# Sketch attention feeding a SiLU MLP on one core: another order of loads and of work, one sixteen-tile pass for the query sketches, and token-major last chunks

## The chip, the cores and the metric

The kernel runs on one core of one Trainium2 chip. The metric is the device time of the whole kernel in microseconds. For the kernel before, 13 runs are shown: median 99.57 us, lowest 98.78 us, highest 100.95 us. In the program's names, PE is TensorE (PEld its weight loads), DVE is VectorE, ACT is ScalarE, POOL is GpSimd, and SP is SyncE, which here only issues DMAs.

## The reference, cut to what matters

```python
def phi(x):                                   # x: 4 x 4 x 1088 x 32, r = 8
    a = np.einsum('rd,bhsd->bhsr', S1, x)
    b = np.einsum('rd,bhsd->bhsr', S2, x)
    return np.einsum('bhsi,bhsj->bhsij', a, b).reshape(*x.shape[:-1], r * r)
q_p, k_p = phi(q), phi(k)
kv  = np.einsum('bhsf,bhsd->bhfd', k_p, v)
z   = np.sum(k_p, axis=2)
num = np.einsum('bhsf,bhfd->bhsd', q_p, kv)
den = np.einsum('bhsf,bhf->bhs', q_p, z)[..., None] + 1e-06
x   = (num / den).transpose(0, 2, 1, 3).reshape(4 * 1088, 128)
h   = x @ w_in                                # w_in 128 x 2048
out = (h * sigmoid(h)) @ w_out                # w_out 2048 x 128, all float32
```

The attention has no softmax: keys and queries are turned into 64 products of two 8-long sketches, and the rest is sums and matrix products. Four batches of 1088 tokens give 4352 rows for the MLP.

## The kernel before, in words

**Two kinds of work share the engines.** The MLP part (`moe_tasks`) takes chunks of 512 or 256 tokens. For each 1024 columns of hidden values PE multiplies x by w_in into one of two double PSUM banks H (line 718), ACT applies SiLU from H to one of eight SBUF tiles G (line 722, 68 times in all), and PE multiplies G by w_out into one of four single PSUM banks B, summing over the hidden dimension (line 729). With the output features on the partitions, DVE transposes B in 32x32 blocks into `ot` (line 734), and four DMAs of 32 partitions each store it (`store_main`, line 690; pieces of 32 floats, 128 bytes). The last 64 tokens of each of the four batches make one common chunk of 256 with eight smaller stores (`store_rest`, line 700).

**The attention part** runs batch by batch: `key_tasks(b)` transposes K in 32x32 blocks (line 299), forms both sketches on PE (`pairs`, line 268), brings them back through DVE (316), forms the outer products on POOL or DVE (322), and from these KV on PE (350 or 372). `z` (328), `zt` (333, ACT), `l2` (336, PE) and `wm` (340, DVE) turn the sum over keys into the matrix WM, masked by head. `query_tasks_hm(b)` for batches 1 to 3 transposes Q (594, 596), forms both query sketches with `proj` (268: eight matmuls on array tiles of 64x32, two heads in one), and, in a second pass, `projm` (606: four matmuls of 128x32 against WM) the vector whose product with the first sketch is the denominator. DVE brings the three back (`back` 618 and 619, `backm` 622 and 623), scales (630 to 633), DVE or POOL forms the outer products (638, or 462 for batch 0), DMAs transpose them (644, on SP), PE multiplies with KV (`num` 650, `numr` 658), and ACT or DVE copies the result to xT, the MLP's input (161, 163). Batch 0 goes through `query_tasks` in smaller pieces, with transposes on PE (483) in place of DMAs.

**Weights and V** come as float32 and are cast to bf16: w_in in four pieces (tasks `cwi0` to `cwi3`), w_out in four (`cwo0` to `cwo3`), V per batch (`vcast`). All are lines 161 (ACT) or 163 (POOL, DVE) of the helper `copy`.

**What sets the order.** Every step is a task of the class `Plan`, with engines that it may use, costs, and the PSUM or G slots that it takes and gives back. The string ORDER, written out, lists the tasks' numbers in the order in which they are emitted, and ".1" after a number chooses the second of the task's engines. `replay` walks through this list with the costs to choose slots; each engine then executes its own instructions strictly in the emitted order. Until the first H, `fill` puts dummy matmuls (line 837) into PE's gaps; their number follows from the costs, not from what happens on the chip. All loads go through SP's queue; in the built program a DMA also waits until the one issued eight DMAs earlier has landed.

Of the kernel before, what the change touches and what calls it, by code (L numbers as in the profile page):

```python
# [16 lines left out]
0 6 73 27 24 1 28 23 2.1 21 3.1 29 32 22 4 96 30 33 7 5 31 10 34 39.1 15 41.0 36 101 35 54 49 47.0  # L17
74 55 50 51 57 75 45.1 43.0 52 58 25.0 56 77 37.0 78 76 59 26.0 60 42 38 142 40 44 61.0 13 46 48
139 66 53.1 67 62 141 97 63.0 9.0 17 103 8.1 68.1 64 99 104 65.0 100 19 79 11.0 225 80 98 228 226
12.0 144 69 182 105 229 140 70.1 86.1 231 143 107 71 106 232 234 81.1 72.1 87 121 113 235 239 14.0  # L20
114 82 240 88.1 108.0 242 83.1 115 89 227 146 16.0 90.0 84 245 116 110.0 85.0 147 122 243 123 111.0
124 246 253 125 18.0 241 126 254 244 127 248 247 249 102.0 230 256 148 130.0 257 20.0 259 128.0 233
131 260 236 250 237 109.0 262 129 251 265 149 263 255 112.0 150 258 238 145.0 152.1 266 117 164 156
118.1 268 151.0 119 252 271 269 120.0 261 190 91.1 264 272 189 154.0 134 184 274 136.1 137.0 183
267 155.0 185 157 270 275 153.1 186 279 132.1 273 280 276 305 277 158 306 282 159 278 191 283 165
193 285 192 167 308 198.0 286 166 168 160 309 169 199 170 288 161.1 307 200 289 311 310 312 281
171.0 291 284 292 173.0 314 172 162 287 315 317 197.0 174 290 318 294 293 295 133 201 320 202 313
163.1 194.1 321 323 187 196.1 316 319 324 195.0 297 177 298 188.0 326 180.1 296 327 179.1 300 322
175.0 301 207 325 331 299 332 334 92 302 335 93.1 357 303 208 358 304 135 360 211 328 210 361 363
329 209 364 337 330 212 359 338 213 366 94 333 367 176 340 336 341 95.1 343 218.0 216.0 203 219 344  # L30
369 339 204.0 370 217 214.0 346 362 347 205 349 206.0 215 138.1 342 350 372 365 373 221 178 375
181.1 224.1 345 376 409 368 410 412 220 413 378 222.1 371 379 223.1 352 411 353 414 383 374 384 386
348 387 389 377 390 380 392 381 385 393 395 382 351 396 398 354 399 401 355 388 402 404 356 391 405
415 394 416 397 423 400 424 426 403 427 418 406 419 429 407 417 430 437 408 420 438 440 421 425 441
422 432 428 433 443 431 444 446 434 447 439 435 442 436 445 448 449 450
# [9 lines left out]
class Plan:  # L45
# [29 lines left out]
    def replay(self, seq):  # L75
        now, mode, queue, port = dict(self.now), None, 4.2, 0.0
# [42 lines left out]
def kernel(  # L119
# [95 lines left out]
    WB4 = const.tile([P, 4, H, R], FP32, name="WB4")  # L215
    hmask = const.tile([P, H], FP32, name="hmask")
# [25 lines left out]
    nc.gpsimd.memset(KV0, 0.0)  # L242
    for t in AW:
        nc.gpsimd.memset(t[:, :, R:], 1e-6)
# [16 lines left out]
    def dma(kb, fn, deps=(), issue=0.44, lag=1.6, due=None, ready=0.0, eng="SP", rate=330.0, name=""):  # L261
        return pl.add(eng, issue, fn, deps, lag=lag, due=due, ready=ready, dq=kb / rate, name=name)
# [9 lines left out]
    def load(b):  # L272
        def lk():
            Kx[b] = tile_x(b, "Kx")
            load_x(nc.sync, Kx[b], k, b, 0, SA)

        def lq():
            Qx[b] = tile_x(b, "Qx")
            load_x(nc.sync, Qx[b], q, b, 0, SA)
        dk = dq = ()  # L280
        if b >= 2:
            dk, dq = ks[b - 2]["kt"], qs[b - 2]["tr"]
        at = (6.2, 24.0, 43.0)[b - 1]
        ks[b]["lk"] = dma(557, lk, dk, due=at, name=f"lk{b}")
        dv = ks[b - 2]["vcs"] if b >= 2 else []
        ks[b]["lv"] = [dma(139, lambda c=c: load_v(nc.sync, b, c), dv, due=at + 0.5, rate=250.0, name=f"lv{b}{c}") for c in range(4)]
        qs[b]["lq"] = dma(557, lq, dq, due=at + 1.0, name=f"lq{b}")

    def key_tasks(b, cuts):
# [41 lines left out]
        def zt():  # L331
            st["zt"] = work.tile([P, HR], FP32, name="zt", tag="zt")
            nc.scalar.activation(out=st["zt"], in_=st["z"][:, 0:HR], func=ACT.Copy)  # L333

# [57 lines left out]
        if b == 0:  # L392
            lv = [dma(139, lambda c=c: load_v(nc.sync, 0, c), due=5.0 + 0.1 * c, rate=250.0, name=f"lv0{c}") for c in range(4)]
# [41 lines left out]
        t = pl.add("PE", 0.22, l2, [t, wts["L2"]], lag=0.22, name=nm("l2"))  # L435
        st["wm"] = pl.add("DVE", 0.2, wm, [t], give=[(tz, 0)], name=nm("wm"))
# [3 lines left out]
        else:  # L440
            k1 = pl.add("PE", 0.42, kv, ou + vc, take=("s",), mode="32", name=nm("kv"))
            t = pl.add(("DVE", "ACT"), (0.23, 0.32), kvm, [k1], name=nm("kvm"))
            t = pl.add("PE", 0.12, kvt, [t], name=nm("kvt"))
# [142 lines left out]
    def query_tasks_hm(b):  # L586
# [11 lines left out]
        def proj(s0, s1):  # L598
            st["p"] = [s0, s1]
            pairs(st["p"], QT, 0, CW)  # L600

        def projm(sl):
            st["m"] = sl
            w = kst["WM"].rearrange("p h r -> p (h r)")
            for c in range(4):
                nc.tensor.matmul(sl[32 * c: 32 * (c + 1), 0:CW], w, QT[:, c, 0:CW], start=True, stop=True,  # L606
                                 tile_position=(0, 32 * c))

        def alloc():
            if "abm" not in st:  # L610
                st["abm"] = work.tile([P, 3, NBX * HR], FP32, name="qabm", tag="qabm")
# [3 lines left out]
        def back(p):  # L615
            alloc()
            dst = st["abm"][:, 0:2, 0:NM].rearrange("p n (h a r) -> p a n h r", h=H, r=R)
            nc.vector.transpose(out=dst[:, :, :, 2 * p: 2 * p + 2, :], in_=st["p"][p][:, 0:NM])  # L618
            nc.vector.transpose(out=st["abm"][:, 0:2, NM + 2 * R * p: NM + 2 * R * (p + 1)], in_=st["p"][p][:, NM:CW])

        def backm():
            nc.vector.transpose(out=st["abm"][:, 2, 0:NM].rearrange("p (h a r) -> p a h r", h=H, r=R), in_=st["m"][:, 0:NM])
            nc.vector.transpose(out=st["abm"][:, 2, NM:CW], in_=st["m"][:, NM:CW])
# [46 lines left out]
        pr = pl.add("PE", 0.61, proj, [t], take=("s", "s"), mode="64", name=nm("proj"))  # L670
        pm = pl.add("PE", 0.54, projm, [t, kst["wm"]], take=("s",), mode="32", name=nm("projm"))
        st["pr"] = [pr, pm]
        ab = [pl.add("DVE", 0.55, lambda p=p: back(p), [pr], give=[(pr, p)], name=nm(f"back{p}")) for p in range(2)]
        m = pl.add("DVE", 0.55, backm, [pm, ab[0]], give=[(pm, 0)], name=nm("backm"))
        sc = pl.add("DVE", scale_cost(9), scale, ab + [m], tt=True, name=nm("scale"))
# [5 lines left out]
        n0 = pl.add("PE", 0.32, num, dm[0:2] + [kst["kvd"]], take=("s", "s"), mode="64", name=nm("num"))  # L681
        n1 = pl.add("PE", 0.09, numr, [dm[2], kst["kvd"]], take=("s",), mode="64", name=nm("numr"))
        st["nums"] = [n0, n1]
        st["xs"] = [pl.add(both, (0.6, 0.62), lambda e, g=g: xcopy(e, g), [n0], give=[(n0, g)], name=nm(f"x{g}")) for g in range(2)]
        st["x8"] = pl.add(both, (0.28, 0.22), xrest, [n1], give=[(n1, 0)], due=T0 + STEP * (16 * b + 12), name=nm("xr"))

    def store_main(b, a0, na, queues):
        def f(ot):
            for r in range(4):
                queues[r % len(queues)].dma_start(  # L690
                    AP(tensor=out.tensor, offset=out[b * S + a0, 32 * r].offset,
                       ap=[[SA * DM, 32], [DM, na], [1, 32]]),
                    ot[32 * r: 32 * (r + 1), 0: 32 * na].rearrange("p (a y) -> p a y", y=32))
        return f

    def store_rest(ot):
        o = ot[:, 0: B * XN].rearrange("p (b c y) -> p b c y", c=NX, y=32)
        for r in range(4):
            for c in range(NX):
                nc.sync.dma_start(  # L700
                    AP(tensor=out.tensor, offset=out[4 * NB + c, 32 * r].offset,
                       ap=[[SA * DM, 32], [S * DM, B], [1, 32]]),
                    o[32 * r: 32 * (r + 1), :, c, :])
# [4 lines left out]
    def moe_tasks(x, n, xdeps, store, nst=4, tag=""):  # L708
# [15 lines left out]
        def o(jp, sl=None):  # L724
            if jp == 0:
                cc["o"] = sl
            for i in range(J):
                j = J * jp + i
                nc.tensor.matmul(cc["o"][:, :n], w_out[:, j, :], view(cc["g", jp], i),  # L729
                                 start=(j == 0), stop=(j == NJ - 1))  # L730

        def tro():
            cc["ot"] = op.tile([P, 512], FP32, name="ot", tag="ot")
            nc.vector.transpose(out=cc["ot"][:, :n], in_=cc["o"][:, :n])  # L734

        prev = xdeps
        last = first = None
        for jp in range(NJ // J):
# [4 lines left out]
            if count[0] == 0:  # L743
# [6 lines left out]
                          take=("s",) if jp == 0 else (), give=[(ts, 0)], due=due + 1.6 * STEP, last=1.0, name=f"{tag}o{jp}")  # L750
            first = first or last
            count[0] += 1
        t = pl.add("DVE", 0.07 + 0.00124 * n, tro, [last], give=[(first, 0)], due=due + 3.5 * STEP, name=f"{tag}tr")
        dma(n * 0.7, lambda: store(cc["ot"]), [t], issue=0.42 * nst, due=due + 6 * STEP, name=f"{tag}st")["last"] = 1.0
# [29 lines left out]
    wts["WB4"] = pl.add(("ACT", "DVE"), (0.84, 0.22), lambda e: wmask(e, WB4, 4, hmask), [t, wts["WP"]], give=[(t, 0)], name="WB4")  # L784
    t = pl.add("PE", 0.3, l2_in, [wts["WB4"]], take=("s",), due=9.0, name="l2in")
# [84 lines left out]
```

## Time and profile before

| what | value |
|---|---|
| median of 13 runs | 99.57 us |
| the profiled execution's own time | 99.96 us |
| its span, first to last instruction | 97.8 us |
| PE busy in the span | 88.2 us (90%) |
| ACT busy in the span | 71.9 us (73%) |
| DVE, POOL busy | 57.7 us, 29.4 us |
| mean of one SiLU (128x1024, line 722), 68 of them | 1032 ns |
| first SiLU starts, last one ends | 17.21 us, 91.09 us |

The times of the lines are counted from the span's start. The span is 2.16 us shorter than the execution's own time; this rest lies around the instructions. Rows of ACT overlap a little, so 68 SiLUs of 1032 ns each are only 65.0 us of busy time.

### The profile page before, as it was taken

Reading aid. Unit: us, or ns where it says so; the run is one execution under the profiler, and the core shown is the slowest. Engines: PE = TensorE matmul, PEld = TensorE weight load, DVE = VectorE, ACT = ScalarE, POOL = GpSimd, SP = SyncE. Lnnn points to the kernel's source line nnn. Section 1 sums busy time; section 2 is a strip of 40 time slices with the busy share of each in tenths; the row PEclk is TensorE's granted clock in tenths of the full one; section 3 lists DMA queues with packets and bytes.
Section 4 is the critical chain, followed back from the end, with each engine's and each line's share of the span. In section 5 each row is a group of like instructions: output and inputs, shape, how many; then the busy total and the mean of one; then the engine's idle time right before and its main releaser. Section 6 shows DMA issues by size and latency. Waiting matters only on the chain.

```text
span 97.8 us, 2280 instructions
## 1 busy us (share of the span) xinstructions
PE 88.2 (90%) x869; PEld 51.7 (53%) x879; DVE 57.7 (59%) x146; ACT 71.9 (73%) x88; POOL 29.4 (30%) x41
## 2 busy tenths in 40 slices
PE   5999989999991999999999999999999999999600
PEld 4545559685841554545554443444564447799400
DVE  4669589997996898379953687992150220210300
ACT  3210266998883579888999999999999999999200
POOL 5019416799469996049100000000000000000000
PEclk9999999999999999999999999999999999999985
DMA  2999999999999944751066505726400066053151
GB/s 51 240 262 211 306 405 310 316 182 236 252 310 163 126 72 89 179 86 32 0 126 127 215 7 89 121 59 132 92 0 0 10 99 106 0 79 61 21 86 28
DMA packets 30874, 12.93 MB, mean 132 GB/s; under 512 B 26256, under 2 KB 29072, under 8 KB 30864
## 3 DMA queue, kind: packets, MB, share of 16 engines
q1 hardware_dynamic: 30240, 12.72, 60.1%
q10 hardware_dynamic: 624, 0.07, 0.5%
q8 instruction: 7, 0.11, 0.5%
q14 instruction: 3, 0.02, 0.1%
HBM read 8.79 MB, written 2.23 MB: 113 GB/s over the span
## 4 chain that ended last, share of the span: by engine, by line
PE 72%; DMA 14%; POOL 4%; ACT 2%; issue 1%; DVE 1%; SPq 0%; POOLq 0%; ACTq 0%
PE B L729 28%; PE H L718 25%; DMA Vf<-in_v_dram 8%; PE B L837 7%; DMA w_outf<-in_moe_w_out_dram 6%; POOL Vh L163 2%; PE H L268 2%; POOL w_out L163 2%; ACT G L722 2%; PE B L372 1%; PE B L328 1%; PE B L606 1%; PE B L268 1%; PE B L650 1%; PE B L539 1%
## 5 line engine op out<-in xcount | busy, mean ns | idle before, releaser
L722 ACT ACTIVATE G<-H 128x1024 bf16<-128x1024 f32 x68 | 65.0, 1032 | 7.8 <-PE H L718 3.2
L729 PE MATMUL B<-G,w_out 128*128 128x512 bf16 (+1 forms) x174 | 37.3, 330 | 2.3 <-POOL w_out L163 2.0
L718 PE MATMUL H<-xT,w_in 128*128 128x512 bf16 (+1 forms) x152 | 36.5, 336 | 0.2
L718 PEld LDWEIGHTS <-w_in 128*128 128x128 bf16 x176 | 18.4, 115 | 12.3 <-issue 3.2
L729 PEld LDWEIGHTS <-w_out 128*128 128x128 bf16 x176 | 17.0, 98 | 12.8 <-POOL w_out L163 2.3
L734 DVE STREAM_TRANSPOSE ot<-B 128x512 f32<-128x512 f32 (+1 forms) x11 | 6.5, 593 | 19.1 <-PE B L729 19.1
L322 POOL TENSOR_TENSOR kp<-kab 128x512 bf16<-128x512 f32 (+1 forms) x15 | 14.7, 1003 | 9.7 <-DVE kab L316 9.7
L837 PE MATMUL B<-zero 128*128 128x256 bf16 x51 | 10.2, 350 | 1.1 <-DVE fmask L231 1.1
L638 DVE TENSOR_TENSOR qp<-aqs,qabm 128x1024 bf16<-128x1024 f32 (+1 forms) x8 | 8.8, 1136 | 0.1
L837 PEld LDWEIGHTS <-zero 128*128 128x128 bf16 x51 | 5.7, 122 | 3.5 <-DVE fmask L231 1.1
L299 DVE STREAM_TRANSPOSE KT<-Kx 128x576 f32<-128x576 f32 (+4 forms) x10 | 6.0, 618 | 1.4 <-DMA Kx<-in_k_dram 1.4
L163 DVE CAST xT<-B 128x512 bf16<-128x512 f32 (+1 forms) x6 | 3.7, 636 | 4.0 <-PE B L650 3.9
L163 POOL CAST Vh<-Vf 128x1152 bf16<-128x1152 f32 x3 | 4.3, 1443 | 2.2 <-DMA Vf<-in_v_dram 2.2
L462 POOL TENSOR_TENSOR qp<-aqs,qabm 128x512 bf16<-128x512 f32 (+1 forms) x4 | 3.8, 959 | 1.6 <-DVE aqs L457 1.6
L594 DVE STREAM_TRANSPOSE QT<-Qx 128x1024 f32<-128x1024 f32 x3 | 3.7, 1233 | 0.8 <-DMA Qx<-in_q_dram 0.8
L322 DVE TENSOR_TENSOR kp<-kab 128x512 bf16<-128x512 f32 (+1 forms) x6 | 4.1, 696 | 0.1
L333 ACT ACTIVATE zt<-B 128x32 f32<-128x32 f32 x4 | 0.8, 208 | 3.8 <-PE B L328 3.8
L163 POOL CAST w_out<-w_outf 128x512 bf16<-128x512 f32 x4 | 3.4, 860 | 0.0
L618 DVE STREAM_TRANSPOSE qabm<-B 128x256 f32<-128x256 f32 x6 | 2.5, 420 | 0.9 <-PE B L268 0.9
L316 DVE STREAM_TRANSPOSE kab<-B 128x288 f32<-128x288 f32 x6 | 2.5, 452 | 1.0 <-PE B L268 1.0
L163 POOL CAST w_in<-w_inf 128x512 bf16<-128x512 f32 x3 | 1.9, 646 | 3.5 <-DMA w_inf<-in_moe_w_in_dram 3.5
L268 PE MATMUL B<-QT,WP 64*32 64x288 f32 (+1 forms) x64 | 2.6, 385 | 0.0
(90 smaller groups left out, 67.8 us busy)
## 6 DMA issues: line engine op xcount, KB each, us to landing
Kx<-in_k_dram SPq DMA_DIRECT2D x3, 544.0 KB, 7.3
Qx<-in_q_dram SPq DMA_DIRECT2D x3, 544.0 KB, 5.1
out_dram<-ot SPq DMA_DIRECT2D x24, 64.0 KB, 2.0
Vf<-in_v_dram SPq DMA_DIRECT2D x8, 144.0 KB, 7.5
Vf<-in_v_dram SPq DMA_DIRECT2D x8, 128.0 KB, 5.9
w_inf<-in_moe_w_in_dram SPq DMA_DIRECT2D x2, 512.0 KB, 7.8
w_outf<-in_moe_w_out_dram SPq DMA_DIRECT2D x4, 256.0 KB, 7.9
out_dram<-ot SPq DMA_DIRECT2D x14, 32.0 KB, 1.7
```

Of the source, the lines that this page charges most:

```text
L163: eng.tensor_copy(out=out, in_=in_)
L268: nc.tensor.matmul(dst[p][32 * c: 32 * (c + 1), lo:hi], WPf[64 * p: 64 * (p + 1), :], srcT[64 * p: 64 * (p + 1), c, lo:hi], start=True, st ...
L299: nc.vector.transpose(out=KT[:, c:c + 2, 32 * lo: 32 * hi], in_=src.rearrange("p c a d -> p c (a d)"))
L322: eng.tensor_tensor(out=st["kp"][:, H * lo: H * hi], in0=_bc(a, 2, R), in1=_bc(bb, 1, R), op=ALU.mult)
L462: eng.tensor_tensor(out=st[f"qp{lo}"], in0=_bc(st["aqs"][:, H * lo: H * hi], 2, R), in1=_bc(bq.rearrange("p a (h r) -> p (a h) r", h=H), 1 ...
L594: nc.vector.transpose(out=QT[:, :, 0: 32 * NB].rearrange("p c (a s) -> p a c s", s=32), in_=Qx[b][:, 0: 4 * NB, :].rearrange("p (a c) d -> ...
L638: eng.tensor_tensor(out=st["qp", i], in0=_bc(st["aqs"][:, g0: g0 + n], 2, R), in1=_bc(grp(1)[:, g0: g0 + n], 1, R), op=ALU.mult)
L718: nc.tensor.matmul(view(sl, i), w_inj[:, (J * jp + i) // 4, (J * jp + i) % 4, :], x, start=True, stop=True)
L722: nc.scalar.activation(out=sl, in_=cc[jp], func=ACT.Silu)
L729: nc.tensor.matmul(cc["o"][:, :n], w_out[:, j, :], view(cc["g", jp], i), start=(j == 0), stop=(j == NJ - 1))
L734: nc.vector.transpose(out=cc["ot"][:, :n], in_=cc["o"][:, :n])
L837: nc.tensor.matmul(hold["bank"][:, 0:256], zero[:, 0:P], zero, start=True, stop=True)
```

## The change

- **Order.** A new ORDER. Of the loads, the second part of batch 0's Q goes ahead of its first part, two of the four V loads of batch 0 and two of batch 1 move from SP's queue to ACT's, and K of batch 2 goes ahead of w_out. In the built program POOL now casts the pieces 0, 1 and 3 of w_out and then piece 3 of w_in ahead of batch 1's V, and ACT casts piece 2 of w_out; the first SiLUs belong to the second chunk of batch 0, not the first. POOL casts part of batch 0's V. `l2` for batches 1 to 3 uses column tiles.
- **Query sketches of batches 1 to 3.** `proj` and `projm` become one pass of sixteen matmuls on 32x32 tiles: one for each head and each group of 32 partitions of the output. The weights are in a new tile WQ: 8 columns for each sketch (from WP, added on POOL, `wq`) and 8 for the summed keys, which `wmh` copies in. It takes one H double bank and two B banks where three B banks were taken in two steps. DVE brings back four pieces (one per head) where it brought three.
- **Last chunks.** The last two chunks of batch 3 and the common rest use G as the stationary side, 128 tokens at a time: eight matmuls of 128 columns where there were four of 256. The output then has tokens on the partitions, so two plain copies (`cpo`, on DVE or ACT) take the place of the transpose, and stores move rows of 512 bytes: four DMAs for each of these chunks, also for the rest, which had eight. Stores go out in pairs, and the last pair of one chunk on ACT's queue.
- The costs that `replay` uses for DMAs and a few tasks are other numbers; the count of dummy matmuls is 54 where it was 51.

```diff
 ORDER = """
...
-    def dma(kb, fn, deps=(), issue=0.44, lag=1.6, due=None, ready=0.0, eng="SP", rate=330.0, name=""):
+    def dma(kb, fn, deps=(), issue=0.47, lag=1.8, due=None, ready=0.0, eng="SP", rate=300.0, name=""):
...
+        def l2h():
+            for h in range(H):
+                nc.tensor.matmul(st["z"][D * h: D * (h + 1), 64:64 + R], L2[:, D * h: D * (h + 1)], st["zt"][:, R * h: R * (h + 1)],
+                                 start=True, stop=True, tile_position=(0, D * h))
+
+        def wmh(eng):
+            copy(eng, WQ[b % 2][:, 2 * R: 3 * R], st["z"][:, 64:64 + R])
...
-            lv = [dma(139, lambda c=c: load_v(nc.sync, 0, c), due=5.0 + 0.1 * c, rate=250.0, name=f"lv0{c}") for c in range(4)]
+            lv = [dma(139, lambda c=c: load_v(nc.scalar if c > 1 else nc.sync, 0, c), due=5.0 + 0.1 * c, rate=230.0,
+                      eng="ACT" if c > 1 else "SP", name=f"lv0{c}") for c in range(4)]
...
-        def proj(s0, s1):
-            st["p"] = [s0, s1]
-            pairs(st["p"], QT, 0, CW)
-
-        def projm(sl):
-            st["m"] = sl
-            w = kst["WM"].rearrange("p h r -> p (h r)")
+        def proj(hs, s0, s1):
+            st["p"] = [hs[:, 0], hs[:, 1], s0, s1]
             for c in range(4):
-                nc.tensor.matmul(sl[32 * c: 32 * (c + 1), 0:CW], w, QT[:, c, 0:CW], start=True, stop=True,
-                                 tile_position=(0, 32 * c))
+                for h in range(H):
+                    nc.tensor.matmul(st["p"][h][32 * c: 32 * (c + 1), 0:CW], WQ[b % 2][D * h: D * (h + 1), :],
+                                     QT[D * h: D * (h + 1), c, 0:CW], start=True, stop=True, tile_position=(D * h, 32 * c))
...
-        pr = pl.add("PE", 0.61, proj, [t], take=("s", "s"), mode="64", name=nm("proj"))
-        pm = pl.add("PE", 0.54, projm, [t, kst["wm"]], take=("s",), mode="32", name=nm("projm"))
-        st["pr"] = [pr, pm]
-        ab = [pl.add("DVE", 0.55, lambda p=p: back(p), [pr], give=[(pr, p)], name=nm(f"back{p}")) for p in range(2)]
-        m = pl.add("DVE", 0.55, backm, [pm, ab[0]], give=[(pm, 0)], name=nm("backm"))
+        pr = pl.add("PE", 0.65, proj, [t, kst["wm"]], take=("h", "s", "s"), mode="16", name=nm("proj"))
+        st["pr"] = [pr]
+        ab = []
+        for h in range(H):
+            ab.append(pl.add("DVE", 0.47, lambda h=h: back(h), [pr] + ab[0:1],
+                             give=[[], [(pr, 0)], [(pr, 1)], [(pr, 2)]][h], name=nm(f"back{h}")))
...
+                if rows:
+                    for t, d in enumerate(cc["or"]):
+                        nc.tensor.matmul(d[:, 0:P], view(cc["g", jp], i)[:, P * t: P * (t + 1)], w_out[:, j, :],
+                                         start=(j == 0), stop=(j == NJ - 1))
+                    continue
...
+        def cpo(eng, t):
+            if "ot" not in cc:
+                cc["ot"] = op.tile([P, 512], FP32, name="ot", tag="ot")
+            copy(eng, cc["ot"][:, P * t: P * (t + 1)], cc["or"][t][:, 0:P])
...
+    def wq():
+        for w in WQ:
+            nc.gpsimd.tensor_tensor(out=w[:, 0: 2 * R].rearrange("p (n r) -> p n r", n=2), in0=WP[:, :, 0, :], in1=WP[:, :, 1, :], op=ALU.add)
...
+            end = b == B - 1 and lo >= 4
+            moe_tasks(xT[b][:, P * lo: P * hi], P * (hi - lo), need, store_rows(b, 4 * lo) if end else store_cols(b, 4 * lo, 4 * (hi - lo)),
+                      rows=end, end=end, tag=f"m{b}{lo}")
```

## The prediction

> **What bounds the kernel now.** I read the page's slices first, then the list of waits for PE and ACT, then the timeline around the largest wait, then the timeline after the last SiLU. The slices (40 of 2.45 us each; a digit is a tenth busy) say that there are three regimes.
>
> ```profile
> PE   5999989999991999999999999999999999999600
> ACT  3210266998883579888999999999999999999200
> DMA  2999999999999944751066505726400066053151
> ```
>
> From slice 8 on PE is full, but for one slice with a 1 (29.3 to 31.8 us), and ACT is full from about 44 us on. DMA is full in the first 32 us: loads set when the early work can start. In the last slices nothing is full. So I price four things apart: when the first SiLU starts (17.21 us), the hole, the stretch in which PE and ACT run side by side, and what follows the last SiLU (91.09 us to 97.8, 6.7 us).
>
> ```profile
> PE B L729 <- POOL w_out L163: 2.0, 1, 2.0
> ACT G L722 <- PE B L729: 2.9, 1, 2.9
> ```
>
> Each line is who waited for whom: total, times, longest. PE stood once, 2.0 us, for a cast of w_out on POOL; ACT, which lives from PE's products, then stood 2.9 us. Both are by far the longest waits after the first SiLU. The timeline of POOL tells why:
>
> ```profile
> 24.96 0.62 POOL L163 CAST w_out<-w_outf 128x512 bf16<-128x512 f32 x1
> 27.79 2.04 POOL L163 CAST Vh<-Vf 128x1152 bf16<-128x1152 f32 x1 [2.21 <-DMA Vf<-in_v_dram]
> 29.78 1.60 POOL L163 CAST w_out<-w_outf 128x512 bf16<-128x512 f32 x1
> ```
>
> Columns are start, duration, engine, line, operation, and in brackets the idle time ahead. The last piece of w_out is queued behind batch 1's V, whose load lands only at 27.7, and both casts are slow: 2.04 us where the same cast takes 1.14 later, and 1.60 where it takes 0.62. PE had its last product at 28.84 + 0.44 = 29.28 and the next at 31.43.
>
> The tail:
>
> ```profile
> 90.00 1.08 ACT L722 ACTIVATE G<-H 128x1024 bf16<-128x1024 f32 x1
> 90.83 1.25 PE L729 MATMUL B<-G,w_out 128*128 128x256 bf16 x10
> 92.12 0.45 DVE L734 STREAM_TRANSPOSE ot<-B 128x256 f32<-128x256 f32 x1 [1.30 <-PE B L729]
> 92.60 0.86 ACTq L690 DMA_DIRECT2D out_dram<-ot  x2
> 92.77 2.84 SPq L690 DMA_DIRECT2D out_dram<-ot  x6
> ```
>
> SP issues six stores in a row after the last transpose: four belong to the chunk before, whose output was ready at 90.83 but stood behind the eight stores of the rest (87.67 to 92.66). The issues end at 95.61, and 2.19 us later the span is over.
>
> **What the Trainium skill says.** (1) "GPSIMD Engine Reference", section 1, Specifications: POOL's SBUF ports are shared with VectorE, with contention when VectorE runs an instruction with two SBUF inputs. The trace agrees: the slow casts lie beside DVE's two outer products (27.60 to 30.91). (2) "TensorEngine Tiling (Array Packing)", Key Properties and Gotcha 1: tiles run independently, a change of mode drains the array, and different row tiles must write different PSUM banks. In the trace eight 64x32 tiles run side by side: 0.65 us for a pass of 288 columns (23.29 to 23.94). No row shows sixteen. (3) "DMA: Bandwidth & Descriptors", Queues, rings and completion order: each DMA engine takes turns between the queues of SP and ACT. So V on ACT's queue doesn't wait behind all of SP's backlog, but takes bandwidth from Q. No row here shows two loaded queues.
>
> **The change part by part.** All against the profiled execution: span 97.8, own time 99.96. The median of 13 is 99.57; I take the difference in us off the median.
>
> *First SiLU: +0.8 us.* I follow the chain in the changed order with the durations of before. PE ends K's second sketch at 7.66. Then 8 dummies of 0.214 (to 9.37), z 0.44, 2 dummies (10.24), second half of Q 0.43, l2 0.34, first half 0.38 (11.39), 3 dummies of 0.143, both projm 0.36 + 0.41 (12.59), 8 dummies (13.73), KV's 18 matmuls 0.93 (14.66). DVE: the first backm after projm at about 12.25, a second one, 0.25 each, scale 1.06 (12.54 to 13.60 before), outer product 0.69: 14.55. ACT: KV out 0.52 (15.33), qt 0.60 (15.93), cast of w_in about 0.55 (16.5), x 0.38 after PE's num at 16.4 (17.0), the issue of a V load about 0.4 (17.4), and then a second qt of 0.60, which stood behind the first SiLUs before: its outer product is on POOL, 15.65 + 1.07 = 16.7, plus 0.3 on PE. SiLU starts at 18.0 against 17.21. If dummies are at 0.11 it is +0.3; if they stay at 0.214, or V's issue on ACT waits for a landing, +1.6. The four issues on ACT: two go into 2.83 us of idle ACT ahead of L2's copy, one into 3.77 us ahead of zt, the fourth is counted. SP loses them and is not the limit, since DMAs are full either way.
>
> *The hole: -2.1 us.* POOL now casts w_out 0, 1, 3 and w_in 3 ahead of V, and ACT casts w_out 2. PE's 29.28 to 31.43 goes (2.15). What is late next: loads added up in queue order, through the last w_out piece, are 5.7 to 5.85 MB in the new order; before, the third w_out load landed at 24.58 after 5.6 MB and the last at 26.83 after 6.1, so now at 25.0 to 25.7. Its cast and that of w_in's last piece are then done by 27. PE needs the latter for the tenth SiLU: 18.0, nine SiLUs at 0.92, 1.7 of copies and a cast on ACT and 0.6 of gaps are 28.6, and the product lies 0.7 ahead of it: 27.9. V of batch 1 lands at 28.2 (6.55 MB), 0.5 later than now, but its cast and one outer product are all that then stand ahead of KV, at about 31.6 where it is 34.1 now. So V is no longer late.
>
> *PE, ACT and DVE in the full stretch: -0.5 us.* Removed from PE: 0.65 + 0.62 for each of three batches. Added: a sixteen-tile pass. At best it costs the eight-tile 0.65, since columns are as many; with 16 more records (a float32 matmul is two) at the pitch (0.65 - 0.41)/15 = 0.016 it is 0.9; I take 0.8, so 3 x 0.47 = 1.4 saved. The worst case, four row groups one after another, is 4 x 0.65 = 2.6. Products of 128 columns:
>
> ```profile
> L483 PE MATMUL B<-identb,qp 128*128 128x128 bf16 x18 | 1.8, 220 | 0.3 <-DVE qp L462 0.3
> L606 PE MATMUL B<-QT,WM 128*32 128x288 f32 x24 | 2.1, 418 | 0.0
> ```
>
> Four of the first kind with weights of their own take (0.40 - 0.22)/3 = 0.06 each to start, so eight are 0.48 where four of 256 columns are 0.44: 12 steps x 0.04 = 0.5 lost. PE gains 0.9. ACT gets a cast (0.62), an x copy (0.60) and a small copy (0.2), and gives up two kvx (0.28) and a KVd (0.31): +0.55. The pass also holds one of two H banks until DVE has taken two of four pieces, 0.8 + 0.2 + 2 x 0.43 + 0.2 = 2.1 us, in which ACT has one bank; its copies to xT lie there and cover most. DVE has one more piece per batch, 0.43: cover is its idle time (it is at 59%), and without it 1.3 us. Together I count half of PE's gain; bounds -1.4 and +1.0.
>
> *The tail: -2.0 us.* After the last SiLU: PE as now, 1.05; copy of 128x128 0.28 on each of DVE and ACT at once (the kvx row) in place of 0.45; a hop of 0.2; two issues on each queue at 0.47, not six: 2.5; then 2.19 as now: 4.7 against 6.7. The rest has four stores, not eight, and the chunk before is out of SP by then: its products end about 1.6 ahead of the last SiLU, copies 0.6, four issues 1.9. Bounds -2.4 and -0.8 (128-column products at 0.11 each, which is 0.4 more in the end and in each step before).
>
> Sum: +0.8 - 2.1 - 0.5 - 2.0 = -3.8: span 94.0, own time 96.2, median **95.8 us**.
>
> **Rivals.** *A, the hole comes back smaller or at another place (97.8 us):* w_in's last piece stands behind w_out's last on POOL. If that lands at 26.8 as now and DVE's products slow both casts to 1.60, PE waits from 27.9 to 30.0, about 2.0. For it: the same port, the same queue; against: less is queued ahead of it than before (5.8 MB, not 6.1), and DVE is then in scale, two of whose four instructions have one input. *B, the gains are paid at both ends (97.2 us):* dummies and waits put the first SiLU at +1.4, and the tail gives 1.2. For it: the chain of the first SiLU has no slack. *C, slower (101.2 us):* the sixteen tiles serialise by row group, on PE, which is full: 3 x (2.6 - 0.8) = +5.4. It decides from 3.8/3 = 1.27 us more in each pass, about 2.1 us a pass. Against: two row groups ran side by side in line 268.
>
> **How the numbers follow.** Forecast 0.62, A 0.18, B 0.11, C 0.09. Low end: 95.8 - 0.9 (all of PE's gain) - 0.5 (start) = 94.4. High end: A with a little of the start, 98.2; C and half of the rest lie outside. A measurement of this kernel tells about 0.5% from no change. Faster by more: the forecast, A and nearly all of B, 0.88; within: 0.03; slower: C, 0.09.
>
> **What would show it.** Right: no wait of PE for w_out beyond 0.5 us; first SiLU near 18.0; line 621's pass at 0.65 to 0.9 us; span less last SiLU near 4.7. Wrong: a wait of PE for w_in's cast or of ACT for a DMA, gaps of ACT over 1 us beside the passes, or SP still issuing 2 us after the last copy.

## The result and the profile after

| | before | after |
|---|---|---|
| median, in the job that timed both | 100.05 us (48 runs) | 98.62 us (11 runs) |
| ratio of after to before, 95% interval | | 0.9888 [0.9849, 0.9927] |
| the profiled execution's own time, its span | 99.96, 97.8 us | 98.62, 96.7 us |
| first SiLU starts, last one ends | 17.21, 91.09 us | 17.57, 91.23 us |

The ratios here and below leave out runs that were more than 1.5% above the fastest of the same kernel; the medians hold all runs. The kernel became faster by 1.1%, not by the forecast 3.8%. 98.62 us lies 2.8 above the forecast of 95.8 and 0.4 above the upper end of its range.

The page's slices of the changed kernel (40 of 2.42 us):

```profile
PE   5999989999998699999993999999999999999900
ACT  3310236999999784999995679999999989999710
DMA  2999999999402922798695000572650341605220
```

The 1 in PE's row is gone. In its place there are a 6 at 31.4 to 33.8 us and a 3 at 50.8 to 53.2. DMA's row now has a 4, a 0 and a 2 at 24.2 to 31.4 us.

POOL's timeline, where the hole came from (start, duration, engine, line, operation, idle time ahead):

```profile
22.25 1.18 POOL L164 CAST w_out<-w_outf 128x512 bf16<-128x512 f32 x2
24.39 0.62 POOL L164 CAST w_out<-w_outf 128x512 bf16<-128x512 f32 x1
26.10 1.15 POOL L164 CAST Vh<-Vf 128x1152 bf16<-128x1152 f32 x1 [0.30 <-DMA Vf<-in_v_dram]
```

w_out is ready at 25.0 us, before V lands, and each cast is quick. PE waits for w_out nowhere. But PE's timeline shows other waits after the first SiLU, in the brackets:

```profile
31.75 0.56 PE L385 MATMUL B<-kp,Vh 128*32 128x64 bf16 x36 [0.64 <-DVE kab L321]
33.55 0.23 PE L395 MATMUL B<-identb,kvx 128*128 128x128 bf16 x1 [0.46 <-DVE kvx L164]
52.84 0.41 PE L661 MATMUL B<-qt,KVd 64*32 64x512 bf16 x8 [1.50 <-DMA qt<-qp]
```

Two lie in batch 1's KV and one ahead of batch 2's `num`. With a wait of 0.25 at 19.5 us they make 2.85 us, more than the 2.0 of the hole.

**The sum, by PE.** The view of busy time by stretch, from the first product of the first SiLU to the last matmul, shows that PE hardly pauses. First the kernel before, then the changed one; the columns are the stretch, its length, then busy time and count for PE, PEld, DVE, ACT and POOL, PE's clock, DMA share and GB/s.

```profile
16.57:92.08 75.51, 72.98 (x693) 42.45 (x701) 45.20 (x94) 66.63 (x77) 22.96 (x25) 1.00 0.57 111
```

```profile
16.78:91.90 75.12, 71.85 (x779) 42.07 (x787) 44.11 (x99) 67.54 (x79) 24.14 (x27) 1.00 0.50 110
```

Some records of matmuls are missing (779 where 787 weight loads are seen), so I take PE's work as the length less the waits that are named: 75.51 - 2.0 = 73.5 before, 75.12 - 2.85 = 72.3 after. Waits too short for the list count as work here. ACT is busy for 67 of 75 us. The difference of these two spans is then complete:

| part | before | after | difference | forecast |
|---|---|---|---|---|
| start of the first product | 16.57 | 16.78 | +0.21 | +0.8 |
| PE's named waits | 2.0 | 2.85 | +0.85 | -2.1 |
| PE's work | 73.5 | 72.3 | -1.24 | -0.5 |
| from the last matmul to the end of the span | 5.72 | 4.80 | -0.92 | -2.0 |
| span | 97.8 | 96.7 | -1.10 | -3.8 |

The tail of the changed kernel, as its timeline shows it, with one line of SP's waits below:

```profile
89.27 1.96 ACT L733 ACTIVATE G<-H 128x1024 bf16<-128x1024 f32 x2
89.88 2.02 PE L743 MATMUL B<-w_out,G 128*128 128x128 bf16 x32
90.07 4.22 SPq L707 DMA_DIRECT2D out_dram<-ot  x6
91.94 0.29 DVE L164 COPY ot<-B 128x128 f32<-128x128 f32 x1 [1.90 <-DMA out_dram<-ot]
92.31 0.85 ACTq L707 DMA_DIRECT2D out_dram<-ot  x2
```

```profile
SPq L707 <- DMA out_dram<-ot: 1.4, 1, 1.4
```

PE, copies and ACT's issues run as the prediction had them, but SP is busy until 94.29: its last issue, at 93.97, first waited 1.4 us for the landing of another store.

These are two single executions. How far such parts vary is told by the first SiLU: it starts between 16.71 and 17.81 us in the profiles of the changed kernel and of the ten variants of it below, so the first row can't be told from no change.

### The profile page after: what moved, and what is told of

The parts are those of the page before. It is cut to its first block, busy times and chain, and to the rows that moved or that the text cites. A ratio compares the mean times of both kernels' runs of the same rounds, so it can differ in the third digit from the quotient of the medians.

```text
span 96.7 us, 2487 instructions
## 1 busy us (share of the span) xinstructions
PE 87.1 (90%) x962; PEld 51.7 (53%) x972; DVE 56.5 (58%) x153; ACT 72.5 (75%) x89; POOL 31.6 (33%) x46
## 4 chain that ended last, share of the span: by engine, by line
PE 44%; DMA 32%; SPq 7%; DVE 7%; ACT 2%; issue 2%; POOL 1%; ACTq 0%; DVEq 0%
PE H L729 20%; PE B L746 17%; DMA Qx<-in_q_dram 12%; DMA Vf<-in_v_dram 11%; DMA qt<-qp 5%; DMA out_dram<-ot 4%; SPq L701 2%; SPq L186 2%; PE B L743 2%; DVE kab L321 2%; SPq L655 1%; DVE qp L649 1%; PE H L621 1%; DVE QT L613 1%; POOL Vh L164 1%
## 5 line engine op out<-in xcount | busy, mean ns | idle before, releaser
L746 PE MATMUL B<-G,w_out 128*128 128x512 bf16 (+1 forms) x125 | 31.4, 352 | 0.3
L746 PEld LDWEIGHTS <-w_out 128*128 128x128 bf16 x128 | 12.2, 97 | 10.2 <-issue 0.7
L751 DVE STREAM_TRANSPOSE ot<-B 128x512 f32<-128x512 f32 (+1 forms) x8 | 5.1, 641 | 11.2 <-PE B L746 11.2
L649 POOL TENSOR_TENSOR qp<-aqs,qabm 128x1024 bf16<-128x1024 f32 (+1 forms) x3 | 4.8, 1593 | 13.9 <-DVE aqs L644 13.9
L649 DVE TENSOR_TENSOR qp<-aqs,qabm 128x1024 bf16<-128x1024 f32 (+1 forms) x6 | 7.9, 1364 | 0.1
L743 PE MATMUL B<-w_out,G 128*128 128x128 bf16 x96 | 6.7, 219 | 0.0
L164 POOL CAST Vh<-Vf 128x1152 bf16<-128x1152 f32 (+1 forms) x4 | 4.0, 1012 | 8.1 <-DMA Vf<-in_v_dram 8.1
L743 PEld LDWEIGHTS <-G 128*128 128x128 bf16 x96 | 6.0, 98 | 0.8
L164 DVE COPY ot<-B 128x128 f32<-128x128 f32 x5 | 1.3, 287 | 7.1 <-DMA out_dram<-ot 4.7
L633 DVE STREAM_TRANSPOSE qabm<-H 128x256 f32<-128x256 f32 x6 | 2.6, 428 | 2.1 <-PE B L621 2.1
```

The source lines that it names most:

```text
L164: eng.tensor_copy(out=out, in_=in_)
L649: eng.tensor_tensor(out=st["qp", i], in0=_bc(st["aqs"][:, g0: g0 + n], 2, R), in1=_bc(grp(1)[:, g0: g0 + n], 1, R), op=ALU.mult)
L743: nc.tensor.matmul(d[:, 0:P], view(cc["g", jp], i)[:, P * t: P * (t + 1)], w_out[:, j, :], start=(j == 0), stop=(j == NJ - 1))
```

## The experiments

**Theory 1** (at first): the lead that the missing hole gives is handed back where x of batch 2 is late, because its transposes stand in SP's in-order queue. It became, with the sum above: PE stops only where it waits for something, so the time is PE's work plus PE's waits. **Theory 2**, the rival: the sixteen-tile pass, which takes one of two H banks, costs ACT its time (ACT stands 1.23 and 0.59 us beside batch 2's pass, 1.04 and 0.34 beside batch 3's), and ACT's gaps set the pace.

All ratios are to the kernel before in the same job; the changed kernel has 0.9888. A profile is one execution, so I read from profiles where waits lie, and take gains from the ratios.

| | edit | median us | ratio, 95% interval |
|---|---|---|---|
| E1 | SP's order | 97.37 | 0.9803 [0.976, 0.9847] |
| E2 | kernel before, w_out cast ahead of V | 99.27 | 0.9926 [0.9889, 0.9963] |
| E3 | query sketches in two passes | 100.18 | 0.9982 [0.9947, 1.0018] |
| E5 | one store for each last copy | 98.47 | 0.9822 [0.9763, 0.9881] |
| E6 | two stores fewer ahead of the last chunk | 95.99 | 0.9697 [0.9619, 0.9775] |
| E8 | one outer product to POOL | 99.5 | 0.9904 [0.9842, 0.9966] |
| E9 | last chunks column-major | 98.9 | 0.9933 [0.9891, 0.9974] |
| E10 | E1, E6 and E8 together | 97.54 | 0.9783 [0.969, 0.9876] |
| E11 | E1 and E6 together | 96.49 | 0.9681 [0.9623, 0.9739] |
| E12 | E11 with another order on DVE | 96.79 | 0.9716 [0.9659, 0.9774] |
| E13 | 16 small activations added on ACT | 98.24 | 0.9848 [0.9782, 0.9914] |

### E1: SP's order

SP's timeline in the changed kernel, with the number of DMAs at the end of each line:

```profile
37.03 1.51 SPq L176 DMA_DIRECT2D Qx<-in_q_dram  x1
38.64 1.33 SPq L190 DMA_DIRECT2D Vf<-in_v_dram  x3
40.06 2.16 SPq L701 DMA_DIRECT2D out_dram<-ot  x4
42.86 1.62 SPq L190 DMA_DIRECT2D Vf<-in_v_dram  x3
44.58 1.86 SPq L701 DMA_DIRECT2D out_dram<-ot  x4
46.54 2.61 SPq L655 DMA_TRANSPOSE qt<-qp  x2
```

The first product for the transposes was ready on POOL at 43.01 us, the second on DVE at 44.97; both stood behind loads and stores.

```diff
 SP, batch 2 (V2 = loads of batch 2's V, V3 of batch 3's)
-Q3, V2 x3, m04 stores x4, V3, V2, V3, m02 stores x4, transposes x2, V3 x2, small transpose
+V2 x4, Q3, m04 stores x4, transposes x2, m02 stores x4, small transpose, V3 x4
```

> The changed kernel with another order on SP's queue only: batch 2's four V loads ahead of the load of batch 3's Q, and batch 2's two large transposes ahead of the stores of one chunk and of batch 3's V loads. Theory 1 (the lead that the missing hole gave was handed back because x of batch 2 is not there, and it is late because its transposes stand in SP's queue behind stores and loads): the transposes start about 43.1 and 45.0 instead of 46.5 and 47.9, ACT's wait of 1.3 us for num goes, SiLU 33 starts near 53.5 instead of 55.97, and the kernel is 1.5 to 2.5 us faster than the changed one (about 96.5). Theory 2 (the sixteen-tile pass, which holds one of two H banks, costs the time): SiLU 33 moves by less than 0.7 and the time stays within 0.5 of the changed kernel's.

Measured: the transposes go out at 43.66 and 46.70, `num` starts at 51.55 without a wait, SiLU 33 at 54.67 rather than 55.97. The ratio fell by 0.0085, about 0.85 us: less than the 1.5 to 2.5 expected. `num` now starts when PE's order comes to it, only 1.3 us earlier than in the changed kernel's profile, and not every execution of the changed kernel has the wait (see the end of the next section). The six runs lie between 96.87 and 97.58 us, where the changed kernel's 11 lie between 97.53 and 100.81. The second product on DVE was ready only at 46.67, since POOL's products had moved beside it; E8 and E10 take this up.

### E2: the hole alone, in the kernel before

```diff
 POOL
-cast w_out 2, cast V of batch 1, cast w_out 3
+cast w_out 2, cast w_out 3, cast V of batch 1
```

> The kernel before with one move: on POOL the last cast of w_out goes ahead of batch 1's V, nothing else. It prices the hole alone. Prediction on record: 2.0 to 2.1 us faster than before. Theory 1 (ACT then runs ahead of batch 2's x, and the lead is handed back there unless the transposes come earlier too): at most 1.0 us faster, with a new wait of ACT or PE for num's operands between 45 and 54 us. Theory 2: nothing takes the lead away, since this kernel has no sixteen-tile pass: 2.0 to 2.9 us faster.

Measured: 0.74% faster. PE's wait for w_out is gone, and another has come at 32.38 us, not between 45 and 54 as theory 1 had it. PE, then DVE, then POOL in the kernel of E2:

```profile
32.38 1.02 PE L729 MATMUL B<-G,w_out 128*128 128x512 bf16 x4 [0.94 <-DVE ot L734]
```

```profile
27.86 4.11 DVE L638 TENSOR_TENSOR qp<-aqs,qabm 128x1024 bf16<-128x1024 f32 x2
28.85 3.61 POOL L322 TENSOR_TENSOR kp<-kab 128x512 bf16<-128x512 f32 x2
```

PE now waits for DVE to empty a bank B, and DVE is held by two outer products, which take 4.11 us beside two on POOL (3.31 before). So the hole had covered DVE's backlog: of 2.0 us of wait, 0.94 came back within a microsecond of where the hole had ended. From the first SiLU to SiLU 33 the profile of E2 is 1.1 us shorter than before, which is the 2.0 less the 0.94. My price of the hole is wrong in the kernel before as well, and neither theory had the place.

### E3: the query sketches as they were

```diff
-pr = pl.add("PE", 0.65, proj, [t, kst["wm"]], take=("h", "s", "s"), mode="16", name=nm("proj"))
+pr = pl.add("PE", 0.61, proj, [t], take=("s", "s"), mode="64", name=nm("proj"))
+pm = pl.add("PE", 0.54, projm, [t, kst["wm"]], take=("s",), mode="32", name=nm("projm"))
...
```

Lines 618 to 623 and 336 to 340 of the kernel before come back with it; `projm` of batches 1 and 3 stands one or two products later on PE than `proj`, so that banks are free.

> The changed kernel with the query sketches of batches 1 to 3 as they were before: eight tiles of 64x32, then four of 128x32, three single banks B in place of the H bank, three pieces brought back by DVE, and the older sum over keys (l2 and wm). All else stays. Prediction's step: PE has about 0.57 us more in each of three batches, so 0.5 to 1.5 us slower than the changed kernel. Theory 1: within 0.5 us, since ACT waits for batch 2's x in either case. Theory 2 (the H bank is what costs): ACT's gaps beside the passes of batches 2 and 3 (1.23, 0.59, 1.04 and 0.34 us) fall below 0.5 in sum each and the kernel is 1 to 2 us faster.

Measured: 0.0094 above the changed kernel's ratio, some 0.9 us slower. Theory 2 wanted it 1 to 2 us faster, with ACT's gaps below 0.5 us. They aren't: without the H bank ACT stands 2.20 us beside batch 2's passes and 0.90 and 1.06 beside batch 3's. So the sixteen tiles, with the smaller sum over keys that goes with them, are the part that brings most of those that I took out alone, and the H bank isn't the cost. The pass in the changed kernel, first and last group, then PE's next product:

```profile
35.63 0.43 PE L621 MATMUL H<-QT,WQ 32*32 32x288 f32 x2
...
35.99 0.41 PE L621 MATMUL B<-QT,WQ 32*32 32x288 f32 x2
36.33 0.42 PE L729 MATMUL H<-xT,w_in 128*128 128x512 bf16 x1
```

Sixteen tiles take 36.33 - 35.63 = 0.70 us, as long as eight of twice the size (0.65).

### E5 and E6: the last stores

E5 sends each last copy of 128x128 as one DMA; E6 does so for the last chunk but one alone, so that two DMAs fewer lie between the last chunk's stores and the eighth ahead of them.

```diff
-eng.dma_start(AP(..., ap=[[SA * DM, 32], [4 * DM, 2], [1, DM]]), ot[32 * c: 32 * (c + 1), 0: 2 * P]...)
+eng.dma_start(AP(..., ap=[[DM, 4], [SA * DM, 32], [1, DM]]), ot[:, P * t: P * (t + 1)])
```

> The changed kernel with the last two chunks of batch 3 stored by two DMAs each, one of 128 partitions for each copied tile of 128x128, where there were four of 32 partitions for both. Of the last chunk one goes out on ACT and one on SP. Theory on the tail (SP's last issue waited 1.4 us for the landing of an earlier store, and two issues on each queue follow one another): no wait at the end, one issue on each queue right after its own copy, 1.3 to 1.9 us faster than the changed kernel. Rival (what ends the kernel is the time that a store takes to land, and a store of 64 KB takes longer than one of 32 KB): the issues end 1.6 us earlier but the last landing comes only 0 to 0.6 us earlier.

> The changed kernel with two stores fewer ahead of the last chunk: the last chunk but one goes out in two DMAs of 128 partitions, the last one keeps its four of 32. Theory (SP's very last issue waited 1.4 us for the store issued eight DMAs earlier, which is one of the last chunk's own on ACT): with two DMAs fewer in between that wait is gone, SP's last issue is at most 0.5 us behind its last but one, and from the last SiLU's end to the end of the span it is 4.2 us, not 5.5: about 1.2 us faster than the changed kernel. Rival (the last landings and what follows them set the end): 5.2 us or more, within 0.3 us of the changed kernel.

Measured in E5: counted from the last SiLU's end (89.92), the issues end after 1.6 us (91.49), where the changed kernel takes 3.1 (91.23 to 94.29). But the span ends only after 95.8 - 89.92 = 5.9 us, 0.4 more than there. The rival was right, and more so than it said. Busy time and DMA by stretch in E5, for a microsecond in which nothing but the two stores runs:

```profile
93.00:94.00 1.00, 0.00 (x0) 0.00 (x0) 0.00 (x0) 0.00 (x0) 0.00 (x0) 1.00 0.25 68
```

A share of 0.25 is that of four of 16 DMA engines. The Trainium skill has this in "DMA: Bandwidth & Descriptors", Rules for kernel authors: the outermost dimension of the pattern bounds how many engines a DMA uses. Mine is 4; the share agrees. E5's better ratio must come from ahead of the tail; in its profile batch 2's transposes were not late, which the edit doesn't touch.

E6, in which the last chunk keeps its stores of 32 partitions:

```profile
87.53 1.96 ACT L739 ACTIVATE G<-H 128x1024 bf16<-128x1024 f32 x2
90.21 0.29 DVE L164 COPY ot<-B 128x128 f32<-128x128 f32 x1 [1.90 <-PE B L749]
90.56 0.80 SPq L713 DMA_DIRECT2D out_dram<-ot  x2
90.58 0.86 ACTq L713 DMA_DIRECT2D out_dram<-ot  x2
```

Both queues are done at 91.4 and the span ends at 94.1, 4.6 us after the last SiLU's end at 89.49 (5.5 in the changed kernel). In the changed kernel SP's very last store (93.97) uses, and waits on, the semaphore of ACT's first store of the same chunk (92.31); with two DMAs fewer it has another, and doesn't wait. The gain in the tail is 0.9 us; the rest of E6's ratio (0.0191 below the changed kernel) lies ahead of the tail: its profile has no wait for transposes and a first SiLU at 16.71, and the edit touches neither.

### E8 and E10: an outer product to POOL

```diff
 q1outer0
-DVE, behind q1outer1
+POOL, behind the cast of batch 1's V and one product
```

> The changed kernel with one of batch 1's two large outer products on POOL, behind its cast of V and one product, where both were on DVE. Theory 1 in its second form (PE never stops from the first SiLU on but where it waits for something, so the time is PE's work plus PE's waits; of these 0.64 us for a bank that DVE's transposes of kab free and 0.46 us for kvx come from DVE's backlog behind the two products): DVE is done with them about 1.5 us earlier, both waits of PE go, and the kernel is 0.8 to 1.1 us faster than the changed one, in its runs without other delay. Theory 2 (ACT's gaps beside the sixteen-tile passes set the time): those gaps stay as they are and so does the time, within 0.3 us. A third outcome is that the two engines slow each other so much that the products on both end no earlier: also no gain.

> The changed kernel with three of the edits together: SP's order with batch 2's V and transposes first, one of batch 1's large outer products on POOL, and two stores fewer ahead of the last chunk. If PE's waits and the last store's wait are what kept the gain away, the sum is 1.2 (the late transposes) + 1.0 + 1.2 us: 95 to 96 us, near the forecast on record. If PE's order and ACT's gaps set the pace, it is no better than the first of them alone, 97.4.

Measured: no gain in E8 (0.9904; by the medians of all runs it is 0.996 of before, where the changed kernel has 0.986), and E10 is no faster than E11, the same kernel without this edit (0.9783 and 0.9681; the intervals overlap). In E8 DVE was done 1.8 us earlier and both waits for batch 1's KV went, as theory 1 said, but a new one of 2.1 us came for `num` of batch 1, whose transpose had to wait for POOL's product (35.49 us, line 661). POOL was late by its own load too: it stood 1.1 us for V.

E10 shows what the two engines do to each other. DVE's and POOL's timelines:

```profile
27.19 1.97 DVE L649 TENSOR_TENSOR qp<-aqs,qabm 128x1024 bf16<-128x1024 f32 x1
29.09 2.44 DVE L327 TENSOR_TENSOR kp<-kab 128x512 bf16<-128x512 f32 x1
```

```profile
26.81 1.27 POOL L327 TENSOR_TENSOR kp<-kab 128x512 bf16<-128x512 f32 x1
28.05 2.93 POOL L649 TENSOR_TENSOR qp<-aqs,qabm 128x1024 bf16<-128x1024 f32 x1
```

Elsewhere DVE's two kinds take 1.23 and 0.68 us and POOL's large one 1.96. Each product here ends when the other engine's product ends, plus its own usual time: DVE's first at 28.08 + 1.2 = 29.3 (measured 29.16), POOL's at 29.16 + 1.96 = 31.1 (30.98), DVE's second at 30.98 + 0.68 = 31.7 (31.53). They take turns. The Trainium skill says so in "SBUF — State Buffer", SBUF: two separate sides: the port pair that the two share is held for a whole instruction when DVE reads two SBUF inputs, and the other engine stands. The trace agrees. Of the outcomes on record for E8, the waits are those of the first and the time is that of the third.

### E9: the last chunks column-major

```diff
-store_rows(b, 4 * lo) if end else store_cols(b, 4 * lo, 4 * (hi - lo))
+store_cols(b, 4 * lo, 4 * (hi - lo))
...
```

The products of 256 columns, the transpose and the eight stores for the rest come back with it.

> The changed kernel with its last two chunks of batch 3 and the common rest column-major again, as in the kernel before: four products of 256 columns for eight of 128, a transpose for two copies, stores in pieces of 128 bytes, eight of them for the rest. The order of the stores and their queues stay those of the change. It prices the token-major chunks alone. Prediction on record: they cost 0.5 us on PE and give 2.0 in the tail, so this would be 1.5 us slower. What the two profiles show (PE 0.6 more for the products, 0.9 to 1.2 less after the last SiLU): 0.3 to 0.7 us slower.

Measured: 0.9933 against 0.9888, so token-major chunks may bring about 0.45%, which isn't clear of noise, as the intervals overlap. From the last SiLU's end it is 96.8 - 90.66 = 6.1 us, 0.7 more than in the changed kernel. On PE the change costs 96 products at 0.057, 5.5 us, for twelve steps at 0.44, 5.3: 0.2, not 0.5.

### E11: the two gains together

```diff
+E1's order on SP
+E6's stores
```

> The changed kernel with two edits together: SP's order with batch 2's V and transposes first, and two stores fewer ahead of the last chunk. The move of one outer product to POOL is left out, since it gave nothing. If the wait for the late transposes and the wait of the last store are separate losses, both gains add: no wait of PE for num's operands over 0.3 us, 4.2 to 4.7 us from the last SiLU's end to the end of the span, 95.5 to 96.3 us in all, and no runs 1.5 us above that. If the first edit only moves the loss to another wait, it is no faster than the second alone, 96.0.

Measured: 0.9681, six runs from 96.04 to 96.67 us. PE's waits in the full stretch are the 0.58 and 0.46 of batch 1's KV and two below 0.3; from the last SiLU's end it is 4.6 us. It beats both kernels and comes within 0.6 points of the forecast's ratio (95.8 of 99.57 is 0.962). E6 alone has a lower median and a ratio that can't be told from it, but one of its six runs is at 97.98.

### E12: batch 1's keys first

```diff
 DVE, batch 1
-q1outer1, q1outer0, k1 product, kab x2, Q transpose of batch 2, kvx, ot, KVd
+q1outer1, k1 product, kab x2, q1outer0, kvx, ot, KVd, Q transpose of batch 2
 PE
-num of batch 1, w_out x2 ...
+w_out x3, num of batch 1 ...
```

> The kernel of the run above with another order on DVE: batch 1's product for the keys and batch 2's key transposes go ahead of the second large outer product of batch 1's queries, the transpose of batch 2's Q goes behind KVd, and on PE num of batch 1 goes behind two more products with w_out. If PE's two waits of 0.64 and 0.46 us (for a bank that kab frees, and for kvx) come only from DVE's order, they go and the kernel is 0.6 to 1.0 us faster than the one above. If DVE and POOL take turns at two-input products, so that the work of both has to be done one after the other in any order, num's transposes come later by what the keys come earlier, and the wait turns up at num: within 0.4 us, or slower.

Measured: no gain over E11. The two waits are gone, as PE's timeline shows (no bracket at L385), and smaller ones stand later:

```profile
31.27 0.56 PE L385 MATMUL B<-kp,Vh 128*32 128x64 bf16 x36
...
35.13 0.41 PE L661 MATMUL B<-qt,KVd 64*32 64x512 bf16 x8 [0.24 <-DMA qt<-qp]
```

```profile
36.34 0.42 PE L621 MATMUL B<-QT,WQ 32*32 32x288 f32 x1 [0.19 <-DVE xT L164]
```

`num` waits for its transposes, and the pass behind it, which needs the banks that `num` holds until x is copied, stops halfway: it takes from 35.47 to 37.03, 1.56 us, not 0.70. What the keys gained, the queries lost.

### E13: more work for ACT

```diff
             nc.scalar.activation(out=sl, in_=cc[jp], func=ACT.Silu)
+            if tag in ("m20", "m24"):
+                nc.scalar.activation(out=warm, in_=hmask[:, 0:1], func=ACT.Copy)
```

> The changed kernel with one tiny activation (128x1, about 0.2 us of ACT) added behind each of batch 2's 16 SiLUs, into a tile that nobody reads: some 2 to 3 us more of ACT, nothing more of PE, in the stretch from 54 to 71 us. If PE's work and waits set the time and ACT's gaps are slack: less than 0.7 us slower than the changed kernel. If ACT sets the pace (theory 2): 2 us slower or more.

Measured: 16 more activations of 250 ns, 4.0 us of ACT between 54 and 75 us, and a median of 98.24 us (98.62 without them). That looks like slack, but the median doesn't settle it: E13's profile has its first SiLU at 16.86 and no wait for transposes, which the edit doesn't touch. ACT's timeline where SiLUs follow one another, first in the changed kernel, then in E13:

```profile
57.33 18.83 ACT L733 ACTIVATE G<-H 128x1024 bf16<-128x1024 f32 x20 [0.34 <-PE H L729]
```

```profile
66.49 1.10 ACT L733 ACTIVATE G<-H 128x1024 bf16<-128x1024 f32 x1
67.39 0.29 ACT L735 ACTIVATE warm<-hmask 128x1 f32<-128x1 f32 x1
67.49 1.11 ACT L733 ACTIVATE G<-H 128x1024 bf16<-128x1024 f32 x1
```

The added activations overlap with the SiLUs: a SiLU follows the last after 1.00 us, where it was (18.83 - 1.02) / 19 = 0.94. So ACT has only about 0.9 us more in 16 SiLUs. From the start of SiLU 33 to the end of the last one E13 takes 90.25 - 54.15 = 36.1 us; the changed kernel takes 35.3, and E1, E5, E6 and E8 to E12 lie between 35.2 and 35.4. So some 0.8 us of the 0.9 arrive at the end: in this stretch ACT is not slack, and part of what I count as PE's work is short waits for ACT: PE's step to the next SiLU's products takes up to 0.27 us in the changed kernel and 0.36 in E13, where 0.22 is usual. Of theory 2, E3 rules out the H bank; that ACT sets the pace in part of this stretch is not ruled out.

## Why the prediction was wrong, step by step

- **What bounds the kernel.** "PE is full, but for one slice with a 1" was right, and it was the key to the sum. So was "ACT is full from about 44 us on": E13 shows that time added to ACT there lengthens the stretch.
- **First SiLU, +0.8.** Measured +0.36, inside the bounds, but variants with the same start spread over 1.1 us, so neither value is confirmed. V's issue on ACT took 0.32 for the 0.4 that I had.
- **The hole, -2.1: the step that failed.** What it says of the hole itself came true: w_out and w_in are cast by 25.0 and 25.8, earlier than the 27 that I had, V lands at 26.1, and batch 1's KV starts at 31.75 for "about 31.6". Wrong is that the whole 2.15 us was booked as a gain. After "So V is no longer late" I looked for the next late thing on POOL and among the loads only. It was on DVE, with two outer products that take turns with POOL's (0.64 and 0.46 us of PE at batch 1's KV; E2 shows the same backlog behind the hole in the kernel before), and then, in the profiled execution, on SP, whose queue held batch 2's transposes (1.5). E2 alone is enough to refute the step: with the hole filled and nothing else changed, the gain was 0.74% (0.4 to 1.1 us), not 2.1 us. Rival A had "the hole comes back smaller or at another place", but named the wrong engine and piece. I cited the shared port for the slow casts, and didn't ask what it does to the products that PE's next steps need.
- **The full stretch, -0.5.** Measured -1.24 of PE's work. A pass costs 0.70, not 0.8, against 1.27 removed; 128-column products cost 0.2 in all, not 0.5. That is -1.5, so most of it counts, not half. E3 puts the pass alone at about 0.9 us. The 2.1 us of one H bank cost nothing that E3, which holds none, gets back. Rival C (tiles serialise) is ruled out by the 0.70.
- **The tail, -2.0.** Measured -1.24 from the last SiLU's end (6.71 to 5.47), -0.92 from the last matmul. "Two issues on each queue at 0.47" missed that SP's second one has to wait for the store whose semaphore it reuses, although I had told of such waits ahead of the prediction; E6 takes 0.9 us of it away and then has 4.6, my 4.7.
- **What would show it.** Of my signs, "gaps of ACT over 1 us beside the passes" came true (1.23 and 1.04), but E3 has such gaps without these passes; "SP still issuing 2 us after the last copy" came true (92.2 to 94.3) and meant what I said.

What stays open: the wait of 1.5 us for batch 2's transposes isn't in every execution. Of seven profiles with SP's order as in the change, those of the changed kernel and E9 have it (1.5 and 1.3 us); of four with E1's order, none. In the changed kernel `num` starts 4.96 us after the issue of the second transpose (47.88 to 52.84), in E5 3.74 us after it and without a wait (47.78 to 51.52). Why the same transpose is late in one execution and not in another, the traces don't tell. Five of the seven lack the wait without E1's order, so that SP's order is its only cause is not shown, and the changed kernel's median holds a share of it that I can't split further. How PE and ACT share the pace after SiLU 33 is open as well.

## What to carry to other kernels

When one engine is full, write the time as that engine's work plus its waits, ask whether a second one is full beside it (here ACT), and before booking a removed wait as a gain, walk each in-order queue that feeds the engine (here DVE, POOL and SP) to the next step that it will ask for: the wait had covered their backlogs. Count products with two inputs on DVE and POOL as one queue, and the last stores with the DMA whose semaphore they reuse.

## What the runs showed of the hardware that I had not expected

- Products with two inputs on DVE and POOL take strict turns: each ended its own usual time after the other's end, within 0.2 us, three times in a row (E10). Moving work between the two gained nothing in E8.
- Small activations of 250 ns, each behind a SiLU, added only about 0.06 us to ACT's pace (0.94 to 1.00 us a SiLU), since they overlap with the SiLUs (E13).
- A pass of sixteen 32x32 tiles of 288 columns took 0.70 us in all three batches, that of eight 64x32 tiles 0.65 before.
- Two stores of 64 KB whose pattern has 4 as its outermost dimension kept the DMA share at 0.25 and 68 GB/s (E5); from the last SiLU's end the issues ended 1.5 us earlier, and the kernel 0.4 us later.
